# A first block of eight token tiles, and a first group on the second weight half that waits slice by slice

## The chip, the core and the metric

The kernel runs on one core of a Trainium2 chip. The metric is device microseconds of one execution. Most executions of one kernel agree within 0.3%, so medians are given with their spread.

## The reference, cut to what matters

Two attention blocks share the input `x` (2048 tokens of 1024 values, bf16); their outputs are mixed by a sigmoid gate.

```python
x = A_x
g = _sigmoid((x * gate_w).sum(-1, keepdims=True))
a = _A_ref(x, A_wqkv, A_wo)      # linear attention, 32 heads
b = _B_ref(x, B_wqkv, B_wo)      # sliding, dilated window of 8
return g * a + (1 - g) * b

# inside _B_ref
qkv = (x @ wqkv).reshape(B, S, 3, H, Dh)   # v is the last third of the columns
```

The kernel starts with the values of block B: `v = x @ wqkv[:, 2048:3072]`. Only this first stage, some 60 of 483 us, is touched by the change.

## The kernel before

The kernel records operations with costs and priorities, orders them with a list scheduler of its own, and emits each engine's instructions with semaphore waits. The first loads and their priorities (lower goes first) are:

```python
load_x(0, 0)                                   # transposing load of token tile 0
load_w(0, 0, Bw, 2048, 0.1, 0, 2, "act")       # first half of the v weights, slices of 2 of 8 row blocks
load_w(0, 0, Bw, 2048, 0.2, 2, 4, "act")
load_x(1, 0.25)
load_w(0, 0, Bw, 2048, 0.3, 4, 6)
load_w(0, 0, Bw, 2048, 0.4, 6, 8)
for t in range(2, NT):
    load_x(t, 3 + t)                           # tiles 2 to 15: priorities 5 to 18
for d in range(0, 8, 2):
    load_w(0, 1, Bw, 2560, 8.1 + 0.1 * d, d, d + 2)   # second half: after tile 5
```

A group is eight matmuls of 128x128 by 128x512 that add up in one result bank. The values are computed in blocks of token tiles, each block first on one weight half, then on the other:

```python
def group(bank, lhs, rhs, reads, lo=0, hi=8):
    ...
    return P.op("pe", fn, (hi - lo) * mm(512), reads=reads, writes=[bank.iv])

for t, half in [(t, half) for b in ((0, 6), (6, 11), (11, NT)) for half in range(2) for t in range(*b)]:
    ...                                        # tiles 0 and 1 on half 0: by slices already
    else:
        bank = main.next()
        o = group(bank, xs, w, [xr, part(0, 8)])     # waits for all it reads
    vt, vs = vst.next()
    move(vt[:, :, 0:32], ..., bank, ...)             # copy by ScalarE or VectorE
    P.op("sp", ..., prio=8.9 if t < 6 and half == 0 else 5)   # store of the copied tile
```

After this come the K and Q projections of B, its windowed attention, block A, and the output projections.

Of the kernel before, what the change touches and what calls it, by code (L numbers as in the profile page):

```python
# [25 lines left out]
class Tile:  # L26
# [16 lines left out]
    def part(self, *idx):  # L43

        dims = list(self.shape[1:])
        strides = []
        s = self.size
        for n in reversed(dims):
            strides.insert(0, s)
            s *= n  # L50
        out = [self.lo]
        for d in range(len(dims) - 1):
            lo, hi = idx[d]
            out = [b + i * strides[d] for b in out for i in range(lo, hi)]
        lo, hi = idx[-1]
        return [(self.space, b + lo * self.size, b + hi * self.size, self) for b in out]
# [1060 lines left out]
def build_kernel(nc, A_x, A_wqkv, A_wo, B_x, B_wqkv, B_wo, gate_w, out):  # L1117
    del B_x
    S = A_x.shape[1]
    NT = S // 128  # L1120
# [7 lines left out]
    def SB(shape, dtype, name, at=None):  # L1128
        n = SZ[dtype]
        for d in shape[1:]:  # L1130
            n *= d
        if at is None:
            at = base[0]
            base[0] += (n + 31) // 32 * 32
        uid[0] += 1
        h = nc.alloc_sbuf_tensor_at("%s_%d" % (name, uid[0]), list(shape), dtype, offset=at)
        return Tile("S", h, at, list(shape), dtype)
# [35 lines left out]
    def hb(p0, p1, half):  # L1173
        return [("H%d" % half, p0, p1, None)]
# [25 lines left out]
    vst = Ring([SB([128, 16, 33], BF16, "vst%d" % i) for i in range(8)])  # L1200
# [38 lines left out]
    def plan(seen):  # L1239
# [72 lines left out]
        Bw = B_wqkv.rearrange("(dc p) f -> p dc f", p=128)  # L1312
# [7 lines left out]
        def load_w(slot, half, src, c0, prio, d0=0, d1=8, eng="sp", after=()):  # L1320
            n = d1 - d0
            return P.op(eng, lambda e: e.dma_start(ws[slot][:, d0:d1, half * 512:half * 512 + 512], src[:, d0:d1, c0:c0 + 512]), 0.4 + 0.2 * n,  # L1322
                        writes=[ws[slot].part((d0, d1), (half * 512, half * 512 + 512))], prio=prio, chan="w%d_%d_%d" % (slot, half, d0), lat=0.55 * n, after=after)
# [7 lines left out]
        for t in range(2, NT):  # L1331
            load_x(t, 3 + t)
        for d in range(0, 8, 2):
            load_w(0, 1, Bw, 2560, 8.1 + 0.1 * d, d, d + 2)
        P.op("sp", lambda e: e.dma_start(gwb[:, :], gate_w[None, :].to_broadcast([128, D])), 0.6, writes=[gwb.all()], prio=29, chan="gw", lat=0.8)


# [2 lines left out]
        def group(bank, lhs, rhs, reads, lo=0, hi=8):  # L1340
            def fn(e):
                last = None
                for dc in range(lo, hi):
                    last = e.matmul(bank.ap(), lhs(dc), rhs(dc), start=(dc == 0), stop=(dc == 7))  # L1344
                return last
            return P.op("pe", fn, (hi - lo) * mm(512), reads=reads, writes=[bank.iv])
# [13 lines left out]
        def x_tile(t):  # L1360
            return (lambda dc: xT[:, dc, t * 128:(t + 1) * 128]), xT.part((0, 8), (t * 128, (t + 1) * 128))

        def x_chunk(u):
            return (lambda dc: xT[:, dc, u * 512:(u + 1) * 512]), xT.part((0, 8), (u * 512, (u + 1) * 512))

        def w_half(slot, half):
            return (lambda dc: ws[slot][:, dc, half * 512:half * 512 + 512]), ws[slot].part((0, 8), (half * 512, half * 512 + 512))

        def w_cols(slot, j):
            return (lambda dc: ws[slot][:, dc, j * 128:(j + 1) * 128]), ws[slot].part((0, 8), (j * 128, (j + 1) * 128))  # L1370

        def move(dst, src, n, bank, reg, scale=None, reads=()):

            if scale is None:
                fd = lambda e: e.tensor_copy(dst, src())  # L1375
                fa = lambda e: e.activation(dst, src(), ACT.Copy)  # L1376
            else:
                fd = lambda e: e.tensor_scalar(dst, src(), scale, None, op0=ALU.mult)
                fa = lambda e: e.activation(dst, src(), ACT.Copy, scale=scale)  # L1379
            P.op("any", {"act": fa, "dve": fd}, {"act": act(n) + (0.1 if reads else 0.0), "dve": dps(n)}, reads=[bank.iv] + list(reads), writes=[reg])  # L1380

        for i in range(WARM):
# [2 lines left out]

        early = {(2, 0): (1, 0, Bw, 1024, 21), (4, 1): (2, 0, Bw, 0, 22), (7, 1): (1, 1, Bw, 1536, 23), (10, 1): (2, 1, Bw, 512, 24),
                 (12, 1): (3, 0, Aw, 1024, 25), (14, 1): (3, 1, Aw, 1536, 26)}
        for t, half in [(t, half) for b in ((0, 6), (6, 11), (11, NT)) for half in range(2) for t in range(*b)]:
            xs, xr = x_tile(t)
            w, wr = w_half(0, half)  # L1390
            part = lambda d0, d1: ws[0].part((d0, d1), (half * 512, half * 512 + 512))
            if half == 0 and t == 0:
                first = [main.next() for _ in range(2)]
                for d in (0, 4, 6):
                    n = 4 if d == 0 else 2
                    for i in range(2):
                        xi, xri = x_tile(i)
                        for c in range(d, d + n, 2):
                            o = group(first[i], xi, w, [xri, part(c, c + 2)], c, c + 2)
                bank = first[0]  # L1400
            elif half == 0 and t == 1:
                bank = first[1]
            else:
                bank = main.next()
                o = group(bank, xs, w, [xr, part(0, 8)])
            vt, vs = vst.next()
            move(vt[:, :, 0:32], lambda bank=bank: bank.ap().rearrange("p (h d) -> p h d", d=32), 512, bank, vt.part((0, 16), (0, 32)))
            P.op("sp", lambda e, t=t, vt=vt, half=half: e.dma_start(vB_hbm[t * 128:(t + 1) * 128, half * 528:half * 528 + 528], vt[:, :, :].rearrange("p h d -> p (h d)")), 0.6, reads=[vt.all()],
                 writes=[hb(t * 128, (t + 1) * 128, half)], chan="vst%d" % vs, lat=0.5, prio=8.9 if t < 6 and half == 0 else 5)
            if (t, half) in early:  # L1410
                load_w(*early[t, half], after=[o])
        load_w(0, 0, Aw, 2048, 30)
# [3 lines left out]
        for t in range(NT):  # L1416
# [4 lines left out]
                 prio=1000 + len(P.ops) + 80)  # L1421
# [131 lines left out]
        for e_ in range(2):  # L1553
            if True:
                for j in range(8):
                    for isq in range(2):
                        for u in (2 * e_, 2 * e_ + 1):
                            bank = main.next()
                            w, wr = w_cols(1 + isq, j)
                            xs, xr = x_chunk(u)  # L1560
# [49 lines left out]
        for t in range(NT):  # L1610
            pkt, _ = pk.next()
            azt, _ = az.next()
            xs, xr = x_tile(t)
            for r in range(4):
                bank = main.next([SO[3]] if r == 2 else [])
                w, wr = w_half((3, 0)[r // 2], r % 2)
# [192 lines left out]
    for _ in range(PASSES):  # L1809
        got = plan(seen)  # L1810
        seen = got[2]
        if best is None or got[0].span < best[0].span:
            best = got
# [56 lines left out]
```

## Time and profile before

| | before |
|---|---|
| time, three runs | 483.5 us median (483.48 to 483.61) |
| time of the profiled run | 484.68 us |
| span in the profile | 482.9 us |
| TensorE busy | 477.1 us, 99% |
| matmul wait for the second weight half | 1.6 us, once |
| K and Q stage starts | 62.83 us |

The lines of the profile that carry the argument stand in the prediction below.

### The profile page before, as it was taken

How to read it: one execution, taken by the hardware profiler on the slowest of the kernel's cores; microseconds unless marked ns; L12 is line 12 of the kernel's file. 1: busy time of each engine (PE TensorE's matmuls, PEld its weight loads, DVE VectorE, ACT ScalarE, POOL GpSimd, SP SyncE). 2: the span in 40 equal slices, each digit the busy share in tenths (PEclk: the TensorE clock that was granted, in tenths of full speed). 3: DMA queues.
4: the chain of work that ended last, by engine and by line, in shares of the span. 5: the costliest groups of instructions: out<-in, count | busy, mean ns of one | idle time of the engine just before them, and what ended most of it. 6: DMA issues, size and time to landing. Idle time of an engine off the chain costs nothing.

```text
span 482.9 us, 10221 instructions
## 1 busy us (share of the span) xinstructions
PE 477.1 (99%) x4403; PEld 224.0 (46%) x4403; DVE 282.7 (59%) x581; ACT 144.9 (30%) x231; POOL 6.2 (1%) x38
## 2 busy tenths in 40 slices
PE   8899999999999999999999999999999999999997
PEld 3344444444444454555454455444444444444443
DVE  3121345799587778565747565688489136653434
ACT  2111111124324345534525334255532130111000
POOL 4000000000000000000000000000000000000000
PEclk9999999999999999999999999999999999999999
DMA  9999993123004336332313447840185018840212
GB/s 207 224 216 305 328 362 112 50 93 97 2 14 149 85 80 162 96 88 54 80 43 88 103 125 163 235 45 2 15 233 146 0 18 241 220 24 2 88 68 88
DMA packets 72950, 57.37 MB, mean 119 GB/s; under 512 B 37953, under 2 KB 60865, under 8 KB 72898
## 3 DMA queue, kind: packets, MB, share of 16 engines
q1 hardware_dynamic: 72210, 56.07, 45.4%
q8 instruction: 35, 0.57, 0.5%
q10 hardware_dynamic: 688, 0.59, 0.4%
q14 instruction: 17, 0.14, 0.1%
HBM read 34.49 MB, written 13.76 MB: 100 GB/s over the span
## 4 chain that ended last, share of the span: by engine, by line
PE 96%; SPq 2%; DMA 1%; issue 0%; DVE 0%
PE ps_all L1344 79%; PE ps_all L1745 11%; PE ps_all L1462 2%; PE ps_all L1497 2%; SPq L1317 2%; DMA w<-in_B_wqkv_dram 1%; PE ps_all L1586 1%; SPq L1322 1%; PE ps_all L1690 0%; PE ps_all L1662 0%; DVE o L1749 0%
## 5 line engine op out<-in xcount | busy, mean ns | idle before, releaser
L1344 PE MATMUL ps_all<-w,xT 128*128 128x512 bf16 x960 | 211.4, 379 | 1.6 <-DMA w<-in_B_wqkv_dram 1.6
L1344 PE MATMUL ps_all<-xT,w 128*128 128x512 bf16 x768 | 168.3, 379 | 0.0
L1344 PEld LDWEIGHTS ps_all<-w,xT 128*128 128x128 bf16 x960 | 92.2, 98 | 112.5 <-DMA w<-in_B_wqkv_dram 2.9
L1344 PEld LDWEIGHTS ps_all<-xT,w 128*128 128x128 bf16 x768 | 74.1, 98 | 89.4 <-issue 1.3
L1745 PE MATMUL ps_all<-w,qT 128*128 128x512 bf16 (+1 forms) x264 | 55.6, 373 | 0.0
L1745 PEld LDWEIGHTS ps_all<-w,qT 128*128 128x128 bf16 x264 | 25.8, 98 | 29.6
L1355 DVE TENSOR_SCALAR e<-e 128x512 bf16<-128x512 bf16 x64 | 18.5, 289 | 32.0 <-ACT e L1353 17.2
L1476 ACT ACTIVATE E<-ps_all 128x1824 bf16<-128x1824 f32 (+1 forms) x18 | 30.4, 1688 | 18.9 <-PE ps_all L1497 18.9
L1375 DVE CAST vst<-ps_all 128x512 bf16<-128x512 f32 x15 | 10.4, 694 | 41.9 <-PE ps_all L1344 41.9
L1749 DVE SCALAR_TENSOR_TENSOR o<-ps_all,gm,xT 128x512 bf16<-128x512 f32 (+1 forms) x25 | 18.0, 728 | 21.1 <-PE ps_all L1745 21.0
L1353 ACT ACTIVATE e<-ps_all 128x512 bf16<-128x512 f32 x32 | 19.1, 597 | 31.4 <-PE ps_all L1344 31.4
L1351 ACT ACTIVATE e<-ps_all 128x512 bf16<-128x512 f32 x32 | 19.1, 597 | 26.1 <-PE ps_all L1344 24.8
L1514 DVE TENSOR_TENSOR ot<-ps_all,rs 128x480 bf16<-128x480 f32 (+1 forms) x54 | 25.8, 506 | 0.0
L1376 ACT ACTIVATE vst<-ps_all 128x512 bf16<-128x512 f32 x17 | 10.2, 600 | 50.4 <-PE ps_all L1344 50.4
L1302 DVE TENSOR_TENSOR mx<-mx,kT 128x1024 bf16<-128x1024 bf16 x32 | 20.9, 685 | 6.5 <-ACT kT L1376 6.3
L1376 ACT ACTIVATE az<-ps_all 128x512 bf16<-128x512 f32 x23 | 13.8, 600 | 36.3 <-PE ps_all L1344 36.3
L1302 DVE TENSOR_TENSOR mx<-mx,qT 128x1024 bf16<-128x1024 bf16 x32 | 21.3, 684 | 4.8 <-ACT qT L1379 4.7
L1376 ACT ACTIVATE kT<-ps_all 128x512 bf16<-128x512 f32 x19 | 11.3, 597 | 38.0 <-PE ps_all L1344 38.0
L1513 DVE RECIPROCAL rs<-ps_all 128x15 f32<-128x15 f32 (+1 forms) x54 | 9.4, 203 | 21.3 <-PE ps_all L1497 19.4
L1357 DVE SCALAR_TENSOR_TENSOR pk<-ps_all,e 128x512 bf16<-128x512 f32 x32 | 21.6, 678 | 0.1
L1379 ACT ACTIVATE qT<-ps_all 128x512 bf16<-128x512 f32 x17 | 10.2, 597 | 34.8 <-PE ps_all L1344 34.7
L1379 ACT ACTIVATE xT<-ps_all,g 128x512 bf16<-128x512 f32 x10 | 6.9, 687 | 45.1 <-PE ps_all L1344 45.1
(73 smaller groups left out, 279.0 us busy)
## 6 DMA issues: line engine op xcount, KB each, us to landing
rb<-rc_hbm SPq DMA_DIRECT2D x32, 256.0 KB, 5.8
w<-in_A_wqkv_dram SPq DMA_DIRECT2D x6, 1024.0 KB, 8.6
v<-vB_hbm SPq DMA_DIRECT2D x36, 132.0 KB, 2.7
vB_hbm<-vst SPq DMA_DIRECT2D x32, 132.0 KB, 6.2
w<-in_B_wqkv_dram SPq DMA_DIRECT2D x4, 1024.0 KB, 9.1
xn<-in_A_x_dram SPq DMA_DIRECT2D x16, 256.0 KB, 2.7
out_dram<-o SPq DMA_DIRECT2D x15, 256.0 KB
oB_hbm<-ot SPq DMA_DIRECT2D x36, 96.0 KB, 2.1
```

The source lines that it names most:

```text
L1302: P.op("dve", lambda e, m=m, op=op: e.tensor_tensor(m[:, 0:n], m[:, 0:n], src, op), 0.08 + n / 1920.0, reads=[m.all(), reg], writes=[m.all()],
L1344: last = e.matmul(bank.ap(), lhs(dc), rhs(dc), start=(dc == 0), stop=(dc == 7))
L1351: P.op("act", lambda e: e.activation(e_[:, :], bank.ap(), ACT.Exp), act(512), reads=[bank.iv], writes=[e_.all()])
L1353: P.op("act", lambda e: e.activation(e_[:, :], bank.ap(), ACT.Exp, accum_out=qe[:, col:col + 1]), act(512) + 0.1, reads=[bank.iv], writes= ...
L1355: P.op("dve", lambda e: e.tensor_scalar(e_[:, :], e_[:, :], 1.0, 1e-6, op0=ALU.min, op1=ALU.add), 0.25, reads=[e_.all()], writes=[e_.all()])
L1357: P.op("dve", lambda e: e.scalar_tensor_tensor(out=dst, in0=bank.ap(), scalar=0.0, in1=e_[:, :], op0=ALU.max, op1=ALU.add), dps(512), read ...
L1376: fa = lambda e: e.activation(dst, src(), ACT.Copy)
L1379: fa = lambda e: e.activation(dst, src(), ACT.Copy, scale=scale)
L1476: P.op("act", lambda e: e.activation(E[:, 0:32 * nq].rearrange("p (j q) -> p j q", j=4), ps[:, 4:8, 0:8 * nq], ACT.Exp), act(32 * nq), rea ...
L1514: P.op("dve", lambda e, r=r, src=src, dst=dst, m=m: e.tensor_tensor(dst, src()[:, :, 0:32], r[:, 0:m, None].to_broadcast([128, m, 32]), AL ...
L1745: last = e.matmul(bank.ap(0, f1 - f0), qT[:, dc, t * 128:(t + 1) * 128], ws[3][:, dc, f0:f1], start=(dc == 0), stop=(dc == 7))
L1749: P.op("dve", lambda e, bank=bank, o_=o_, t=t, n=n, i0=i0, i1=i1, tgt=tgt, c0=c0: e.scalar_tensor_tensor(out=o_[:, i0 * 128:i1 * 128].rear ...
```

## The change

TensorE has no work between the end of the first block and the landing of the second weight half. The change intends to fill that hole in two ways: it puts two more token tiles on the half that is there already, and it lets the first group on the second half start when the first quarter of it has landed. The loads of tiles 6 and 7 have to go ahead of the second half for this, so its priority moves from 8.1 to 10.1, and that of the early stores with it.

```diff
-            load_w(0, 1, Bw, 2560, 8.1 + 0.1 * d, d, d + 2)
+            load_w(0, 1, Bw, 2560, 10.1 + 0.1 * d, d, d + 2)
...
-        for ... for b in ((0, 6), (6, 11), (11, NT)) for half in range(2) for t in range(*b)]:
+        for ... for b in ((0, 8), (8, NT)) for half in range(2) for t in range(*b)]:
...
-                o = group(bank, xs, w, [xr, part(0, 8)])
+                step = 2 if t == 0 else 8
+                for d in range(0, 8, step):
+                    o = group(bank, xs, w, [xr, part(d, d + step)], d, d + step)
...
-                 ..., prio=8.9 if t < 6 and half == 0 else 5)
+                 ..., prio=10.9 if t < 8 and half == 0 else 5)
```

More of the change, by code (lines that the diff above doesn't have):

```diff
@@ L1387, in plan @@
                  (12, 1): (3, 0, Aw, 1024, 25), (14, 1): (3, 1, Aw, 1536, 26)}
-        for t, half in [(t, half) for b in ((0, 6), (6, 11), (11, NT)) for half in range(2) for t in range(*b)]:
+        for t, half in [(t, half) for b in ((0, 8), (8, NT)) for half in range(2) for t in range(*b)]:
             xs, xr = x_tile(t)
@@ L1408, in plan @@
             P.op("sp", lambda e, t=t, vt=vt, half=half: e.dma_start(vB_hbm[t * 128:(t + 1) * 128, half * 528:half * 528 + 528], vt[:, :, :].rearrange("p h d -> p (h d)")), 0.6, reads=[vt.all()],
-                 writes=[hb(t * 128, (t + 1) * 128, half)], chan="vst%d" % vs, lat=0.5, prio=8.9 if t < 6 and half == 0 else 5)
+                 writes=[hb(t * 128, (t + 1) * 128, half)], chan="vst%d" % vs, lat=0.5, prio=10.9 if t < 8 and half == 0 else 5)
             if (t, half) in early:
```

## The prediction

> **What bounds the kernel now.** I read the page's busy shares first, then the chain that ended last.
>
> ```profile
> PE 477.1 (99%) x4403; PEld 224.0 (46%) x4403; DVE 282.7 (59%) x581; ACT 144.9 (30%) x231; POOL 6.2 (1%) x38
> ...
> PE 96%; SPq 2%; DMA 1%; issue 0%; DVE 0%
> ```
>
> The columns are busy microseconds, share of the 482.9 us span and instructions. TensorE is busy 99% of the span, and the chain of waits is 96% TensorE. Only the first 3% of the chain, the DMA queue (SPq) and one transfer, is anything else. Read in order of time, its start says where that is:
>
> ```profile
> 7.95 1.31 SPq L1317
> 9.30 1.31 SPq L1317
> 10.65 0.58 SPq L1322
> 11.28 0.47 SPq L1322
> 11.79 0.47 SPq L1322
> 12.30 5.58 DMA w<-in_B_wqkv_dram
> 17.93 112.41 PE ps_all L1344 x520
> ```
>
> The columns are start, length, what. L1317 issues a transposing load of one token tile, L1322 a load of a weight slice. The chain runs through the issue of token tiles 4 and 5 and of three slices of the second weight half; the fourth is issued at 12.30 and lands 5.58 us later, at 17.88. At 17.93 TensorE starts, and from there to 480.04 the chain has matmuls without a gap. So all that any change of order can win lies before 17.93. TensorE's timeline shows it:
>
> ```profile
> 5.55 10.76 PE L1344 MATMUL ps_all<-w,xT 128*128 128x512 bf16 x48
> 17.93 42.26 PE L1344 MATMUL ps_all<-w,xT 128*128 128x512 bf16 x195 [1.62 <-DMA w<-in_B_wqkv_dram]
> ```
>
> The 48 matmuls are token tiles 0 to 5 on the first weight half. Then TensorE sits idle for 1.62 us until the second half has landed. The list of who waited for whom has no other matmul wait of note in the whole run:
>
> ```profile
> PE ps_all L1344 <- DMA w<-in_B_wqkv_dram: 1.6, 1, 1.6
> PE ps_all L1383 <- DVE warm L1290: 1.3, 1, 1.3
> ```
>
> (total us, times, longest; the second is the warm-up at the very start). The weight loads show the small waits inside the first 48 matmuls:
>
> ```profile
> 9.22 6.59 PEld L1344 LDWEIGHTS ps_all<-w,xT 128*128 128x128 bf16 x32 [0.36 <-DMA xT<-in_A_x_dram]
> 17.93 11.99 PEld L1344 LDWEIGHTS ps_all<-w,xT 128*128 128x128 bf16 x57 [2.11 <-DMA w<-in_B_wqkv_dram]
> ```
>
> From 9.22, when token tile 2 arrived, 32 matmuls (tiles 2 to 5) run with no further wait.
>
> **What the Trainium skill says.** "TensorE: Matmul & The Clock Gate", section "Back-to-back issue gap", gives a warm gap of N / 2.4 + 2.5 ns, about 216 ns at N = 512, and on the same page some 131 ns for a sustained stream. This trace has the first: ScalarE's copies of every second group start at 19.87, 23.32 and 26.77, so 16 matmuls take 3.45 us, 216 ns each and 1.73 us a group. The 379 ns in the matmul rows is a latency. "Perfetto Trace Analysis", section "DMA Instruction — HWDGE (DVE, Sync)", says that the profiled window of such a DMA leaves out the data movement; here the slices' issues take 0.47 to 0.58 us and the last lands 5.58 us after its start. "DMA: Bandwidth & Descriptors", section "Issuing engines are not separate DMA queues", says that all transfers run on the same 16 DMA engines and interleave. That agrees: the first slice landed 3.6 us after issue; the medians of neighbouring pairs (4.4, 5.3, 5.5) put the others at about 5.2, 5.4 and 5.6, while three 132 KB stores, issued from 12.88 on, moved beside them.
>
> **The change part by part.** The order of instructions on TensorE and the SP queue, before and after, shows no matmul added or taken away; from the K and Q projections on TensorE's order is the same.
>
> 1. The hole. At a steady 216 ns the 32 matmuls from 9.22 end their issue at 9.22 + 32 x 0.216 = 16.13. The restart is at 17.93, so the loss is 1.80 us (the profile's 1.62 counts from the end of the last matmul's latency). This is the most that the change can win.
>
> 2. Two more groups ahead of the second half (tiles 6 and 7, first half): 2 x 1.73 = 3.46 us of work moved forward, so the second half is first needed at 16.13 + 3.46 = 19.59.
>
> 3. Two more transposing loads ahead of the slices on the SP queue. The six before took 1.24 to 1.84 us each to issue, mostly 1.31 with the gap between: 2 x 1.35 = 2.7 us later. Slices are then issued at 13.3, 14.0, 14.5 and 15.0, and with the old landing times (3.6, 5.2, 5.4, 5.6) land at about 16.9, 19.2, 19.9 and 20.6. The stores are behind the slices as before, but five go out together, about 0.66 MB in place of 0.4, so I don't assume faster landing.
>
> 4. The wait by slices. Instead of all four before the first matmul, each pair of matmuls waits for its slice: needed at 19.59, 20.02, 20.45 and 20.89. Margins are 2.7, 0.8, 0.5 and 0.3 us: no stall. With one wait for all, the group would start at 20.6, about 1.0 us late. So of 1.8 us, the block is worth 0.8 and the slices up to 1.0.
>
> 5. Tiles 6 and 7 themselves are needed at 16.13 and 17.86. Issued at 10.65 and 11.96, and with the 4.1 us that is the median landing of the transposing loads, they arrive at 14.8 and 16.1; with their longest, 5.6, at 16.3 and 17.6. At worst 0.2 us is lost.
>
> 6. Later loads move. The first halves of K and Q weights stay near 36 to 39 us, one second half comes earlier and the other later (after the 27th group, at about 52), and first use of second halves is after four columns of the K and Q stage, some 25 us after it starts at 60. Hidden. Stores are pushed together behind these 1 MB loads, but a staging buffer is reused only eight groups (13.8 us) later and there are seven result banks.
>
> Sum: 483.5 - 1.8 = 481.7 if all of it is won. I allow 0.2 us for an odd slow issue, which gives **481.9 us**, a gain of 0.33%.
>
> **The rivals.** *The wait comes back smaller.* One transposing load of the first six took 1.84 us to issue instead of 1.31, and later ones, beside other traffic, 2.06 and 2.47. If both new ones take 1.85, all slices move by 1.1 us more; the last then misses its need by 0.8 us and the time is 482.5. For it speaks that the DMA engines are near full from 12.2 us on; against it, that the slow issues came when stores or slices were in the queue, while the new loads stand ahead of both. *Token tiles 6 or 7 become the wait.* They follow straight behind tile 5, whose predecessors already arrived just in time (tile 2 was waited for). A loss of 0.2 to 0.6 us, time 481.9 to 482.3. Against it: loads are issued every 1.35 us and consumed every 1.73 us, so the lead grows. *More than the hole is won or lost elsewhere.* SP's later order changes, and 1 MB loads hold its queue for up to 4.77 us at a store. To stop TensorE, this would have to eat more than ten microseconds of buffering, and TensorE waits for no copy anywhere in the trace. I give it little; it would bring 483.5 or more.
>
> **Range and chances.** The floor is the full hole, 481.7, less 0.2 for noise and for small waits inside the first 48 matmuls: 481.5. The upper end is the first rival with some company: 482.7. All outcomes lie within 0.5% of 483.5, and 2% would be 9.7 us, five times the hole: 0.994 for within 2%, 0.003 each for the others.
>
> **What would show it.** In the changed profile the list of waits should have no matmul wait for w over 0.5 us; the chain should turn to TensorE at 5.5 to 9.3 us and not at 17.93; 64 matmuls should run from 5.55 to about 19.8 and the next follow at once; the slices should be issued from about 13.3 on. Step 3 is wrong if they start after 14; step 5 is wrong if a wait for xT stands between 14 and 20 us. The prediction fails if a wait above 1 us stands at the first group of the second half, or one for a copy or a weight load shows up between 35 and 130 us.

## The result, and the profile after

The changed kernel took 482.77 us (median of six, 482.33 to 483.07), the kernel before in the same rounds 483.56 (its six runs: 483.31 to 484.68). The ratio is 0.9979, 95% interval 0.9967 to 0.9992. Ratios here are those taken from runs of the same rounds, so not quite the ratio of the medians quoted. The gain is about half of what was foretold.

The two profiles, however, differ by about as much as was foretold. The first lines of the chain that ended last in the changed kernel (start, length, what):

```profile
3.61 3.79 DMA w<-in_B_wqkv_dram
7.45 6.67 PE ps_all L1344 x30
14.18 10.74 PE ps_all L1344 x49
24.97 10.74 PE ps_all L1344 x49
```

The chain turns to TensorE at 7.45 us, with a slice of the *first* weight half, and no longer at 17.93. The pieces of 49 matmuls are an artefact: the page counts 4354 matmuls for 4403 weight loads, so 49 records are missing (in this stage every fiftieth), and 26 of them look like an idle 0.16 us. That is also all there is in the changed kernel's list of matmul waits:

```profile
PE ps_all L1344 <- issue: 4.1, 26, 0.2
PE ps_all L1383 <- DVE warm L1290: 1.3, 1, 1.3
```

The wait for `w` is gone. The timeline of the DMA queue answers to step 3 of the prediction: six transposing loads in a row, then the four slices, then five stores.

```profile
4.75 8.56 SPq L1317 DMA_TRANSPOSE xT<-in_A_x_dram  x6
13.36 2.12 SPq L1322 DMA_DIRECT2D w<-in_B_wqkv_dram  x4
15.59 2.59 SPq L1410 DMA_DIRECT2D vB_hbm<-vst  x5
```

By the trace's landing times the slices arrived at 17.63, 18.26, 19.80 and 20.53. TensorE's weight loads run on through all of that. (A weight load, PEld in the profile, goes before each matmul with its 128x128 operand; here that is a block of a token tile, not of the weights `w`.)

```profile
8.20 0.65 PEld L1344 LDWEIGHTS ps_all<-w,xT 128*128 128x128 bf16 x4 [0.21 <-DMA w<-in_B_wqkv_dram]
9.20 20.84 PEld L1344 LDWEIGHTS ps_all<-w,xT 128*128 128x128 bf16 x98 [0.34 <-DMA xT<-in_A_x_dram]
```

From 9.20 there is one unbroken row; before, it broke off at 15.81 and went on at 17.93. The start of the K and Q stage and the last copy to the output show where the gain is. Before:

```profile
62.83 1.46 PE L1344 MATMUL ps_all<-xT,w 128*128 128x512 bf16 x6
...
480.04 0.48 DVE L1749 SCALAR_TENSOR_TENSOR o<-ps_all,gm,xT 128x256 bf16<-128x256 f32 x1 [0.39 <-PE ps_all L1745]
```

After:

```profile
61.01 67.50 PE L1344 MATMUL ps_all<-xT,w 128*128 128x512 bf16 x306
...
478.31 0.48 DVE L1751 SCALAR_TENSOR_TENSOR o<-ps_all,gm,xT 128x256 bf16<-128x256 f32 x1 [0.39 <-PE ps_all L1747]
```

The stage starts 1.82 us earlier, the last copy 1.73 us earlier: what is won in the first stage is kept to the end, within 0.1 us. The signs that the prediction had named all came. (L1749 is L1751 after, as the change adds two lines.) The two profiled runs took 484.68 and 483.07 us, 1.61 apart. The medians are 0.79 apart. That is the riddle that the experiments had to solve.

### The profile page after: what moved, and what is told of

It reads as the page before. It is cut to its first block, busy times and chain, and to the rows that moved or that the text cites. A ratio compares the mean times of both kernels' runs of the same rounds, so it can differ in the third digit from the quotient of the medians.

```text
span 481.3 us, 10169 instructions
## 1 busy us (share of the span) xinstructions
PE 471.5 (98%) x4354; PEld 224.0 (47%) x4403; DVE 281.4 (58%) x578; ACT 146.9 (31%) x234; POOL 6.2 (1%) x38
## 4 chain that ended last, share of the span: by engine, by line
PE 97%; issue 1%; DMA 1%; SPq 1%; DVE 0%
PE ps_all L1344 80%; PE ps_all L1747 11%; PE ps_all L1499 2%; PE ps_all L1464 2%; PE ps_all L1588 1%; DMA w<-in_B_wqkv_dram 1%; SPq L1317 1%; PE ps_all L1692 0%; PE ps_all L1664 0%; DVE o L1751 0%
## 5 line engine op out<-in xcount | busy, mean ns | idle before, releaser
L1344 PE MATMUL ps_all<-w,xT 128*128 128x512 bf16 x934 | 206.9, 379 | 3.2 <-issue 2.5
L1344 PE MATMUL ps_all<-xT,w 128*128 128x512 bf16 x750 | 165.6, 379 | 2.0 <-issue 1.6
L1751 DVE SCALAR_TENSOR_TENSOR o<-ps_all,gm,xT 128x512 bf16<-128x512 f32 (+1 forms) x25 | 18.0, 728 | 21.1 <-PE ps_all L1747 20.9
L1376 ACT ACTIVATE kT<-ps_all 128x512 bf16<-128x512 f32 x21 | 12.6, 598 | 36.8 <-PE ps_all L1344 36.8
L1379 ACT ACTIVATE qT<-ps_all 128x512 bf16<-128x512 f32 x19 | 11.4, 598 | 35.3 <-PE ps_all L1344 35.3
```

Source lines behind the costliest of these rows:

```text
L1344: last = e.matmul(bank.ap(), lhs(dc), rhs(dc), start=(dc == 0), stop=(dc == 7))
L1376: fa = lambda e: e.activation(dst, src(), ACT.Copy)
L1379: fa = lambda e: e.activation(dst, src(), ACT.Copy, scale=scale)
L1751: P.op("dve", lambda e, bank=bank, o_=o_, t=t, n=n, i0=i0, i1=i1, tgt=tgt, c0=c0: e.scalar_tensor_tensor(out=o_[:, i0 * 128:i1 * 128].rear ...
```

## The experiments

**Theory A**: the hole is not the same in every run. It ends when the last slice lands; that moment varies, and the profile of before happened to show a late one. The change wins the hole, which is usually smaller. **Theory B**: the hole is 1.8 us in every run, and the changed kernel usually gives part of it back in a later stage. Twelve experiments were run, in three sets of four; each set ran on one chip, beside its own runs of the kernel before.

### First set: both kernels again, and each half of the change alone

*The kernel before, unchanged.*

> The kernel before, unchanged. Theory A (the profiled run of before was a long one, 484.68 us against 483.31 to 483.70 for the other five; the hole before the second weight half is usually smaller): in a profile of a run near 483.5 us, TensorE restarts at about 17.0 in place of 17.93, a hole of 0.6 to 1.0 us. Theory B (the hole is 1.8 us in every run and part of the gain is given back later in the changed kernel): the hole is 1.6 to 1.8 us again although the run takes 483.5.

*The changed kernel, unchanged.*

> The changed kernel, unchanged. Both theories: 482.3 to 483.1 us, ratio about 0.998. Theory A: no wait above 0.3 us anywhere after the first 9 us, and the spread between its runs lies in when the first loads land (5 to 9 us). Theory B: a wait of about 0.9 us between 20 and 480 us.

*The block of eight alone.*

```diff
-                step = 2 if t == 0 else 8
+                step = 8
```

> Only the block of eight; the first group on the second half waits for all four slices. By the prediction's step 4 this group starts 1.0 us late (all slices at 20.6, needed at 19.59). Theory A, in which loads usually land about 1 us earlier than in the profiled run of before: 0 to 0.3 us late, time within 0.3 us of the changed kernel. Theory B: 1.0 us slower than the changed kernel.

*The slices alone*, in the kernel before:

```diff
-                o = group(bank, xs, w, [xr, part(0, 8)])
+                step = 2 if t == 0 else 8
+                for d in range(0, 8, step):
+                    o = group(bank, xs, w, [xr, part(d, d + step)], d, d + step)
```

> Only the wait by slices, with blocks of six as before. With the landing times of the profiled run of before, the slices at 14.3, 16.5, 17.2 and 17.9 are needed at 16.13, 16.56, 17.0 and 17.43: about 0.45 us late, so 1.35 of 1.8 us won. Theory A: usually no wait, time within 0.3 us of the changed kernel. Theory B: 0.5 us slower than the changed kernel.

| first set, five runs each | median us | range | ratio to before (interval) |
|---|---|---|---|
| before, beside them (nine runs) | 483.74 | 483.54 to 484.65 | |
| before, again | 483.91 | 483.76 to 484.25 | 1.0001 (0.9988 to 1.0015) |
| changed | 483.17 | 482.84 to 483.41 | 0.9987 (0.9973 to 1.0000) |
| block only | 483.51 | 483.26 to 483.84 | 0.9992 (0.9979 to 1.0006) |
| slices only | 482.90 | 482.57 to 483.15 | 0.9978 (0.9965 to 0.9992) |

The new profile of before, weight loads:

```profile
5.92 0.15 PEld L1344 LDWEIGHTS ps_all<-w,xT 128*128 128x128 bf16 x1 [0.18 <-issue]
6.34 0.15 PEld L1344 LDWEIGHTS ps_all<-w,xT 128*128 128x128 bf16 x1 [0.28 <-issue]
6.77 0.15 PEld L1344 LDWEIGHTS ps_all<-w,xT 128*128 128x128 bf16 x1 [0.28 <-issue]
...
17.15 12.85 PEld L1344 LDWEIGHTS ps_all<-w,xT 128*128 128x128 bf16 x61 [0.58 <-DMA w<-in_B_wqkv_dram]
```

Two things differ from the first profile. The second half lands at 17.11, not 17.88, so TensorE restarts at 17.15. And the first matmuls come one per 0.43 us, not one per 0.216, until 7.18 us; the block of six therefore ends later. Both narrow the hole: from matmul start to matmul start, less 0.216 us, it is 0.26 us here and was 1.79 in the first profile. The hole was expected at 0.6 to 1.0 us; it was smaller. Theory A foretold the direction; Theory B foretold 1.6 to 1.8 and falls with this line and with the changed kernel's second profile, which has no wait between 9 us and the end either (K and Q stage from 61.08, last matmul over 417.1 us later; in all fourteen profiles it is 417.0 to 417.3).

The changed kernel, expected at 482.3 to 483.1, is a little above that. Slices alone gain as much as the whole change (0.84 us under the median of before, against 0.57). The block alone gained 0.23 us, an amount whose interval includes zero; it is 0.34 us behind the changed kernel, where Theory A expected at most 0.3. Yet its one profile has no hole:

```profile
6.35 23.70 PEld L1344 LDWEIGHTS ps_all<-w,xT 128*128 128x128 bf16 x110 [0.28 <-issue]
```

In that run the last slice landed at 19.73, early enough: the first matmul on the second half started at 20.01. In the three profiles of the changed kernel the slice landed at 20.53, 20.48 and 19.78, and that matmul started at 19.57, 19.64 and 19.48; a group that waits for all would have been late in all three. That this is why the block alone gains less in its other runs is an argument, not something that a trace showed.

### Second set: late slices, and no warm-up

*Late slices with one wait.* Blocks of six, TensorE's order pinned to that of before, but tiles 6 and 7 loaded ahead of the slices. This is the loss side of the change without its remedy.

```diff
-            load_w(0, 1, Bw, 2560, 8.1 + 0.1 * d, d, d + 2)
+            load_w(0, 1, Bw, 2560, 10.1 + 0.1 * d, d, d + 2)
...
-                o = group(bank, xs, w, [xr, part(0, 8)])
+                o = group(bank, xs, w, [xr, part(0, 8)], after=[o])
...
-                 ..., prio=8.9 if t < 6 and half == 0 else 5)
+                 ..., prio=10.9 if t < 6 and half == 0 else 5)
```

(`group` passes `after` on, which keeps TensorE in program order. Without it the scheduler itself moved tile 6 into the first block.)

> Kernel before with blocks of six in the old order on TensorE (pinned), but token tiles 6 and 7 loaded ahead of the four slices, as in the changed kernel. Theory A (the landing of the last slice sets the end of the run, microsecond for microsecond, as soon as it is later than the end of the first block): slices land at 19.7 to 20.5 us as in the three traces with that order, TensorE restarts there, 2.6 to 3.4 us after 17.1, time 486.3 to 487.3 us. Theory B (the loss is in the change's later order, not in this hole): under 485.

*The same with a wait per slice*, the `step` loop of above with `after=[o]`.

> The same late slices, and the first group waits slice by slice. Theory A: six of its eight matmuls (6 x 0.216 = 1.3 us) run ahead of the last slice's landing, so 1.3 us less than with one wait: 485.0 to 486.0 us. Rival (a wait per slice costs TensorE as much as it saves, in restarts): within 0.3 us of one wait.

*The kernel before, and the changed one, with `WARM = 0` in place of `WARM = 11`*: without the eleven matmuls that keep TensorE busy from 1.25 us until data arrives.

> Kernel before without the eleven warm-up matmuls. The rate of the first matmuls (one per 0.43 us at first, 0.216 later) then changes late. Theory A: TensorE works through tiles 0 to 5 at half rate for some microseconds, catches up with the loads, and the hole before the second half closes by itself: 0.3 to 1.7 us slower than before, 484 to 485.5, with a hole under 0.5 us in the trace.

> Changed kernel without the warm-up matmuls. Theory A: with nothing left to fill, it loses more than before does, 1.3 to 2.6 us, and lands within 0.3 us of the kernel before without warm-up: the change is worth the hole and nothing else. Rival (the change wins by something else than the hole): it stays 0.8 us ahead of the kernel before without warm-up.

| second set, four runs each | median us | range | ratio to before (interval) |
|---|---|---|---|
| before, beside them (seven runs) | 483.93 | 483.35 to 484.59 | |
| late slices, one wait | 488.28 | 488.02 to 488.73 | 1.0091 (1.0074 to 1.0108) |
| late slices, four waits | 485.76 | 485.25 to 487.00 | 1.0044 (1.0026 to 1.0062) |
| before, no warm-up | 484.88 | 484.26 to 485.64 | 1.0015 (0.9997 to 1.0033) |
| changed, no warm-up | 484.71 | 484.26 to 485.68 | 1.0020 (1.0004 to 1.0037) |

Late slices cost more than expected, 4.35 us over before. The profile says why. The expected part is there: the last slice lands at 19.47, TensorE restarts at 19.52. Then something else happens (weight loads of that run):

```profile
19.52 0.55 PEld L1344 LDWEIGHTS ps_all<-w,xT 128*128 128x128 bf16 x4 [3.22 <-DMA w<-in_B_wqkv_dram]
20.25 0.15 PEld L1344 LDWEIGHTS ps_all<-w,xT 128*128 128x128 bf16 x1 [0.18 <-issue]
20.67 0.15 PEld L1344 LDWEIGHTS ps_all<-w,xT 128*128 128x128 bf16 x1 [0.27 <-issue]
21.10 0.15 PEld L1344 LDWEIGHTS ps_all<-w,xT 128*128 128x128 bf16 x1 [0.28 <-issue]
...
23.59 6.36 PEld L1344 LDWEIGHTS ps_all<-w,xT 128*128 128x128 bf16 x30 [0.21 <-issue]
```

For 3.4 us matmuls come one per 0.43 us. The table of stretches of the same run has the granted clock (the third column from the right):

```profile
16.40:19.50 3.10, 0.39 (x2) 0.00 (x0) 0.69 (x1) 0.00 (x0) 0.00 (x0) 1.00 1.08 350
19.50:20.20 0.70, 0.68 (x3) 0.31 (x4) 0.00 (x0) 0.00 (x0) 0.00 (x0) 0.93 1.11 343
20.20:23.60 3.40, 3.40 (x10) 1.22 (x9) 0.00 (x0) 0.60 (x1) 0.00 (x0) 0.51 1.21 226
23.60:27.00 3.40, 3.40 (x17) 1.56 (x16) 0.69 (x1) 0.40 (x1) 0.00 (x0) 1.00 1.23 133
```

A hole of 3.11 us between matmul starts was followed, 0.7 us later, by 3.4 us at a granted clock of 0.51. All four runs of this kernel have a mean granted clock of 0.996, and all seven of before beside them 0.999 or 1.000, so this was no accident of one run. The Trainium skill, "TensorE: Matmul & The Clock Gate", section "What's actually happening", describes such a step down after an idle window of about 3.4 us; here it came after 2.73 us of idle TensorE. The slow matmuls cost 1.7 us (the excess of their spacing over 0.216, added up in the trace). With it the sum closes: restart 19.52, plus the 466.75 us that this kernel needs from its restart to the end (see the third set), plus 1.68, is 487.95; the run took 488.02.

With four waits the last slice landed at 20.20, later than in the run with one wait, but only two matmuls stood behind it, and the clock stayed:

```profile
17.64 0.11 PEld L1344 LDWEIGHTS ps_all<-w,xT 128*128 128x128 bf16 x2 [1.21 <-DMA w<-in_B_wqkv_dram]
18.31 0.11 PEld L1344 LDWEIGHTS ps_all<-w,xT 128*128 128x128 bf16 x2 [0.55 <-DMA w<-in_B_wqkv_dram]
19.50 0.11 PEld L1344 LDWEIGHTS ps_all<-w,xT 128*128 128x128 bf16 x2 [1.08 <-DMA w<-in_B_wqkv_dram]
20.24 4.64 PEld L1344 LDWEIGHTS ps_all<-w,xT 128*128 128x128 bf16 x23 [0.62 <-DMA w<-in_B_wqkv_dram]
```

This is how a wait per slice looks: two weight loads, a wait, two weight loads. The median is 2.5 us better than with one wait. (The slowest of the four runs, 487.00 us, alone has a mean granted clock of 0.996, as the runs with one wait have; it was not traced, but the clock seems to have stepped down there too.) In the two profiles the K and Q stage starts at 66.11 and 63.85, 2.26 us apart: the 1.3 us expected, plus 1.68 for slow matmuls that did not occur, less 0.73 for the later landing. So the rival, that the waits themselves cost as much, falls.

Without the warm-up the runs show no gain: 484.88 and 484.71, ratios 1.0015 and 1.0020 with wide overlap. In that profile of before the hole has closed by itself:

```profile
11.03 0.15 PEld L1344 LDWEIGHTS ps_all<-w,xT 128*128 128x128 bf16 x1 [0.28 <-issue]
11.44 11.54 PEld L1344 LDWEIGHTS ps_all<-w,xT 128*128 128x128 bf16 x54 [0.26 <-issue]
```

TensorE reached the second half so late that it was there. Going by the ratios, the loss of the warm-up cost the changed kernel 1.6 us (1.0020 against 0.9987 in the first set) and the kernel before 0.7. This is what Theory A foretold, that the change is worth the hole and nothing when there is none. It is not shown firmly: each kernel has four runs that spread over 1.4 us, so neither a gain of 0.6 us nor the rival's 0.8 is ruled out. (The profile of before without warm-up ran at half rate until 11.44, that of the changed kernel until 8.53; so single runs of these two can't be compared, only their medians.)

### Third set: how large is the hole, usually?

*The kernel before twice more, one look each.*

> Kernel before, one more profile. In the two profiles so far the time of that run is TensorE's restart on the second weight half plus 466.75 us (17.93 gave 484.68, 17.15 gave 483.91). Theory A: the same sum within 0.2 us, with the restart between 16.7 and 17.9 as the last slice lands.

> Kernel before, a fourth profile: restart plus 466.75 us within 0.2 us again; a run near 483.5 us has its restart near 16.75 and a hole under 0.7 us.

*The changed kernel, and the slices alone, once more.*

> Changed kernel: 0.6 to 0.9 us under before. Its start of the K and Q stage lies between 60.9 and 61.6, by the moment at which the first matmuls change from one per 0.43 us to one per 0.216 us and by the first loads.

> Slices alone, blocks of six: if the block of eight adds nothing once the waits are by slice, within 0.3 us of the changed kernel, as in the first set (482.9 against 483.17). If the block is needed: 0.3 us or more behind it.

All four profiles of the kernel before, the longest run first. Restart is the first weight load on the second half; the hole is counted between matmul starts, less 0.216 us:

| last slice lands | issue to landing | restart | hole | time of the run | time less restart |
|---|---|---|---|---|---|
| 17.88 | 5.58 | 17.93 | 1.79 | 484.68 | 466.75 |
| 17.11 | 4.97 | 17.15 | 0.26 | 483.91 | 466.76 |
| 16.95 | 4.64 | 16.99 | 0.54 | 483.79 | 466.80 |
| 16.46 | 4.33 | 16.50 | 0.00 | 483.26 | 466.76 |

The last column is constant within 0.05 us. In the first three rows the time of the kernel before follows the landing of its last slice. In the last row the landing came as the first block ended (the first matmul on the second half started at 16.57, without a gap), so there TensorE's own work set the time as well; its restart, 16.50, is earlier than the 16.7 that was expected. The hole is anything from nothing to 1.8 us; its mean is 0.65. What makes the transfer slower in one run than in another was not examined. The chain of the run with 483.79 us, to be held against the one that the prediction was read from:

```profile
12.31 4.63 DMA w<-in_B_wqkv_dram
16.95 0.04 issue
16.99 3.19 PE ps_all L1344 x14
```

The same instruction, issued within 0.01 us of the same moment, landed 0.93 us earlier. The three gains between medians are 0.79, 0.57 and (third set, 483.56 less 483.07; expected were 0.6 to 0.9) 0.49 us, 0.62 on average. That is close to the mean hole, but no proof that the hole is all of the gain: the hole comes from four profiled runs that took 483.91 us on average, longer than the medians of before, and the three profiled runs of the changed kernel (482.94 on average) are 0.97 us under these four.

In the third set the changed kernel had 483.07 us (482.79 to 483.11), ratio 0.9991 (0.9977 to 1.0004), and the slices alone 482.89 (482.72 to 483.02), ratio 0.9987 (0.9973 to 1.0000), with 483.56 of before (nine runs, 482.91 to 484.22). Twice, slices alone were 0.2 to 0.3 us ahead of the whole change. That is within the intervals, so no version is called better than the other; but once the waits are by slice, the runs show no worth of the block of eight.

One thing stays open. In all three profiles of the changed kernel the matmul rate doubled at about 4.5 us; in the nine other profiles with warm-up it did so between 5.1 and 7.2. The changed kernel's K and Q stage started at 61.01, 61.08 and 60.92, that of slices alone at 61.51 and 61.30, which the late doubling would explain. It bears on the gain as well: the start of this stage in the kernel before, less its hole, is 61.04, 61.80, 61.36 and 61.47 (in the order of the table), on average 0.4 us later than with the change. So of the 1.06 us between the mean starts in the profiles, 0.65 is the hole and 0.4 lies in the work before it. But the time from that start to the end of the run varied by 0.4 us the other way (421.64 and 421.72 with slices alone, 421.76 to 422.06 with the change); part of this lies after the last matmul, from where the span goes on for 2.83 and 2.86 us with slices alone and for 2.89 to 3.06 with the change. Whether the kernel has any influence on the moment of doubling or the three early ones were chance, and what the 0.4 us are, was not tested.

## Why the prediction was right or wrong

**The mechanism was right, the gain too large by a factor of two.** Foretold were 481.9 us, range 481.5 to 482.7, from a base of 483.5. Measured were 482.77 against 483.56; the ratio 0.9979 applied to 483.5 gives 482.5. The median itself lies 0.07 us above the range. The range reached so far up for a slow issue of the new loads, which did not occur; that it holds the scaled result is luck. Nearly all of the probability was on "within 2%", where it belongs.

- **Where the bound is: right.** In all fourteen profiles, of eight kernels, the time from the start of the K and Q stage to the end of the last matmul was 417.0 to 417.3 us: whatever moved the end by more than some tenths of a microsecond had happened before 66 us.
- **Step 1, the hole, is the term that was mis-sized.** It says that 1.80 us "is the most that the change can win" and the sum subtracts it from 483.5. The 1.80 was read correctly from the profile, but the profiled run had taken 484.68 us. A hole of one run was subtracted from the median of others. From its own run the sum would have been 484.68 - 1.80 = 482.9. Four profiles measure the hole at 0 to 1.79, mean 0.65. The warning was in the table of times before the prediction was made.
- **Step 2, two groups are 3.46 us: right.** Groups follow each other every 1.73 us in the changed kernel as before.
- **Step 3, the slices 2.7 us later: right.** Foretold issue 13.3, 14.0, 14.5, 15.0, measured 13.36, 13.98, 14.50, 15.01; the last landing foretold at 20.6, measured at 20.53.
- **Step 4, no stall, right; the split into 0.8 for the block and 1.0 for the slices, wrong.** It shared out a hole of 1.8. For a usual hole the slices suffice alone (482.90 and 482.89), and six of eight matmuls ahead of the last landing, 1.3 us, are more than that hole.
- **Step 5, tiles 6 and 7 in time: right.** They landed at 14.68 and 15.70, needed at 16.13 and later.
- **Step 6, later loads hidden: right.** No matmul waits for a weight load after 9 us.
- **The rivals.** "The wait comes back smaller" did not occur in the changed kernel; in the two kernels with late slices it did. "Won or lost elsewhere" did not occur. The rival that mattered was missing: that the hole differs from run to run. Missing too was the rate of the first matmuls, which decides when the first block ends and so how large the hole is.

## What to carry to other kernels

A profile is one execution: compare its own time with the median before a wait read from it is subtracted from anything, and take some more profiles when the wait is the end of a transfer. Cutting one wait into one per slice moves only the work of the last slice behind the last landing, and it costs nothing that showed here; try it before reordering work. And a change that fills a hole can be expected to win the hole of a usual run, not that of the run that was profiled; here the hole also shrank when the work ahead of it got slower. To test that the hole is all that is won, compare the profiles of many runs of both kernels: four against three left 0.4 us unexplained here.

## What the Trainium skill lacked or had wrong

- "TensorE: Matmul & The Clock Gate", section "Back-to-back issue gap": its 131 ns for a sustained stream at N = 512 was not seen; hundreds of matmuls in a row ran at 216 ns, its figure for an isolated one (which the same page also reports for back-to-back matmuls, in an earlier section).
- The same page, section "What's actually happening": it asks for an idle window of about 3.4 us before the clock steps down. Here 2.73 us of idle TensorE (3.11 us between matmul starts) was followed by 3.4 us at a granted clock of 0.51; a hole of 1.79 us was not.
- The same page, in the same section, says that the rise of the clock varies by about 0.5 us from run to run, though its own counts of slow matmuls there differ by more. With the first warm-up matmul at 1.25 us, the spacing changed from 0.43 to 0.216 us at moments from 4.5 to 7.2 us. A table of stretches prints a granted clock of 1.00 for the slow matmuls before it, but the trace has no clock record there: in the 12 profiles that have one, it begins with the change of spacing (4.46 us in the first profile of the changed kernel, 7.17 where the spacing changed at 7.18).
- "DMA: Bandwidth & Descriptors", section "Latency and other measured facts", gives no spread for one transfer from run to run: the same 256 KB slice, issued at 12.13 to 12.31 us in four runs of one program, landed 4.33 to 5.58 us later.
- No page says that a profile shows one execution, and that a wait in it can be far from the usual one (1.79 us against a mean of 0.65 in four).
